# Weight conversion in a fused attention, DFT and MLP kernel: the sign as a byte written by ScalarE, the exponent change in ScalarE's scale

## The chip, the cores and the metric

The kernel runs on one core of one Trainium2 chip. The metric is the device time of one execution in microseconds (us); lower is better. The engines that the text speaks of are PE (TensorE: matmuls, with PEld for the loading of its stationary operand), DVE (VectorE), ACT (ScalarE), POOL (GpSimd) and SP (SyncE, which issues the DMAs).

## The reference

Four batches of causal attention with 12 heads give `x`. The real part of a two-dimensional DFT of `x` is added to it, each row is normalised, and an MLP with 768 inputs and 3072 hidden units follows, with a residual.

```
attn_out = softmax(mask(q @ k.T / 8)) @ v            # 4 x 12 heads, 448 x 64
x   = attn_out as [4, 448, 768]
u   = x + real(fft(fft(x, axis=1), axis=2))
un  = (u - mean(u)) / sqrt(var(u) + 1e-6)
out = u + relu(un @ w_ch1) @ w_ch2   # w_ch1 [768, 3072], w_ch2 [3072, 768]
```

The two weight arrays reach the kernel as 64-bit floats, and it makes 32-bit floats of them itself.

## The kernel before, in words

**Stages.** From 0 to about 240 us PE works through 24 pairs of heads, and in between through the DFT, the normalisation and the transposes of the batches that are ready. From about 240 us it works through the MLP: two groups of 896 tokens, each with 12 chunks of 256 hidden units. For a chunk the first product (`f1`, matmuls of 448 columns, written `h`) is followed by the second (`f2`, matmuls of 384 columns, written `o`), and the plan weaves `f2` of a chunk with `f1` of the next. Each matmul is done three times, with operands that are split into a high and a low part. In the first group a plain chunk has 72 matmuls in `f1`, a chunk from number 5 on, counted from 0, has 63 (a recursion with seven products, `fast`), and each has 84 in `f2`. After six matmuls of `f2` DVE adds the PSUM tile into an accumulator in SBUF (L1168); there are 14 such adds for a chunk of the first group, called a **round** here.

**The weights.** The first group converts them, in 48 pieces of 128 x 768 numbers, two of `w_ch1` and two of `w_ch2` for a chunk. A piece arrives by DMA as pairs of 32-bit words, tile `w`: `w[:, :, 0]` the low word and `w[:, :, 1]` the high word of each 64-bit float. Five operations in `weights()` make 32-bit floats of it: ACT writes the magnitude of the high word, read as a 32-bit float, to `w32` (L742), and ACT replaces the low word by its top three bits, from its top byte (L746). DVE joins those bits and the sign bit in the high word (L752), caps the magnitude and changes its exponent (L758), and shifts it by three and joins the rest (L762). The result stays in `w32`. From it come high and low parts: for `w_ch2` by ACT (L775, tile `w2h`) and POOL (L779); for `w_ch1` by `split` and `combine` (`w1` and `ws` tiles, L811 and L824 on DVE or POOL, casts at L335 on ACT). The second group loads what the first has stored.

**What sets the order.** A planner (`Plan.order`) takes a list of units, each with an engine or a choice of engines, a cost and a priority, and writes out a fixed order for every engine before anything runs; engines then go through their lists in order and wait on semaphores. Units with two engines named, such as L811, L824, L905, L930 and L1108 (DVE or POOL), go where the planner thinks that they end first. A cost or a dependency that is changed anywhere can therefore move instructions everywhere behind it. PSUM tiles come from eight banks; the `c` copies (L335, ACT or DVE) take an `h` product out of its bank, and the product that follows into that bank waits for them.

Of the kernel before, what the change touches and what calls it, by code (L numbers as in the profile page):

```python
# [9 lines left out]
F32 = mybir.dt.float32  # L10
F32R = mybir.dt.float32r
BF16 = mybir.dt.bfloat16
U32 = mybir.dt.uint32
U8 = mybir.dt.uint8
ACTF = mybir.ActivationFunctionType
ALU = mybir.AluOpType
AX = mybir.AxisListType.X
# [2 lines left out]
B, H, S, D = 4, 12, 448, 64  # L20
# [28 lines left out]
SLOW, BIAS = 1.5, dict(S=-300, V=-100, G=-500)  # L49
BIG = float(2 ** 30)  # L50
W_SCALE = 2.0 ** -112
W_HIGH = float(np.uint32((1151 << 20) - 1).view(np.float32))
ORDER = (
    [2 * j for j in range(R)]
    + [2 * j + 1 for j in range(R)]
# [20 lines left out]
class Plan:  # L76
# [11 lines left out]
    def add(self, eng, cost, prio, fn, rd=(), wr=(), phase=None):  # L88

        n = len(self.units)  # L90
        deps = sorted({w for r in rd for w in self.writers[r]})
        for x in wr:
            self.writers.setdefault(x, []).append(n)
        for x in set(z[:2] for z in (*rd, *wr)):
            self.uses.setdefault(x, []).append(n)
        many = isinstance(eng, tuple)
        self.units.append(dict(
            n=n, engs=dict(zip(eng, cost)) if many else {eng: cost}, many=many, prio=prio, fn=fn, deps=deps, phase=phase,
            new=sorted({z[:2] for z in wr if z[0] in self.bufs}, key=str)))
# [165 lines left out]
def tile_kernel(ctx, tc, qk, vv, w1, w2, cc, cd, cs, out):  # L265
    nc = tc.nc if tc else None
    T = {}
# [42 lines left out]
    add = plan.add  # L310
# [7 lines left out]
    def dve(n, rate=0.96):  # L318
        return 69 + n / rate
# [4 lines left out]
    def acts(n):  # L324
        return 94 + n * 0.833
# [62 lines left out]
    def attend(i):  # L388
# [50 lines left out]
        for k, rows in enumerate(rows_):  # L439
# [23 lines left out]
            for y, r in enumerate(rows):  # L463
                for h, ps in enumerate(banks):
# [7 lines left out]
                    def f(ps=ps, c0=at[r], n=n, rr=rr):  # L472
                        nc.scalar.activation(  # L473
                            out=T[pb][:, PO[rr]:PO[rr] + n], in_=T[ps][:, c0:c0 + n], func=ACTF.Exp, scale=-1.0,
                            bias=T[mn][:, rr:rr + 1], accum_out=T[sm][:, rr:rr + 1])
# [247 lines left out]
    def weights(j, nm, half, p0):  # L723
        g, c = items[j]
        id_ = (j, half)
        if twice(j):
            if half and not (nm == "1" and kept(j)):
                w = ("w", (nm, j))

                def f():  # L730
                    nc.sync.dma_start(out=wide(w), in_=dr["wf"][int(nm) - 1, c])
                add("D", dma(786432), p0 - 3000, f, rd=[("wf", nm, c)], wr=[w], phase="W")
            return
        w, w32, wh, wl = ("w", (nm, j, half)), ("w32", (nm, j, half)), ("w2h", id_), ("w2l", id_)

        def f():
            src = (w1 if nm == "1" else w2)[2 * c + half]
            nc.sync.dma_start(out=T[w], in_=src.bitcast(U32).rearrange("p (a b) -> p a b", b=2))
        add("D", dma(786432), p0 - 3000, f, rd=[("go", W_FROM)] if j == 0 else [], wr=[w], phase="W")

        def f():
            nc.scalar.activation(out=T[w32].bitcast(F32), in_=T[w][:, :, 1].bitcast(F32), func=ACTF.Abs)  # L742
        add("S", acts(768) + 71, p0, f, rd=[w], wr=[(*w32, 0)], phase="W")

        def f():
            nc.scalar.activation(  # L746
                out=T[w][:, :, 0], in_=T[w].bitcast(U8)[:, :, 3], func=ACTF.Copy, scale=1 / 32, bias=-31 / 64)
        add("S", acts(768) + 75, p0 + 1, f, rd=[w], wr=[(*w, 1)], phase="W")

        def f():  # L750
            x = T[w][:, :, 1]
            nc.vector.scalar_tensor_tensor(  # L752
                out=x, in0=x, scalar=0x80000000, in1=T[w][:, :, 0], op0=ALU.bitwise_and, op1=ALU.bitwise_or)
        add("V", dve(768) + 4, p0 + 2, f, rd=[(*w, 1), (*w32, 0)], wr=[(*w, 2)], phase="W")

        def f():
            x = T[w32].bitcast(F32)
            nc.vector.tensor_scalar(out=x, in0=x, scalar1=W_HIGH, scalar2=W_SCALE, op0=ALU.min, op1=ALU.mult)  # L758
        add("V", dve(768, 1.92) + 4, p0 + 2, f, rd=[(*w32, 0)], wr=[(*w32, 1)], phase="W")

        def f():
            nc.vector.scalar_tensor_tensor(  # L762
                out=T[w32], in0=T[w32], scalar=3, in1=T[w][:, :, 1], op0=ALU.logical_shift_left, op1=ALU.bitwise_or)
        add("V", dve(768) + 4, p0 + 4, f, rd=[(*w32, 1), (*w, 2)], wr=[(*w32, 4)], phase="W")

        if not (nm == "1" and kept(j)):
            def f():
                nc.sync.dma_start(out=dr["wf"][int(nm) - 1, c, :, half], in_=T[w32].bitcast(F32))
            add("D", dma(393216), p0 + 5, f, rd=[(*w32, 4)], wr=[("wf", nm, c)], phase="W")

        if nm == "2":
            wide_lo = (*w32, 4)

            def f():
                nc.scalar.copy(out=T[wh], in_=T[w32].bitcast(F32))  # L775
            add("S", acts(768), p0 + 5, f, rd=[wide_lo], wr=[wh], phase="L")

            def f():
                nc.gpsimd.tensor_tensor(out=T[wl], in0=T[w32].bitcast(F32), in1=T[wh], op=ALU.subtract)  # L779
            add("G", gps(768), p0 + 6, f, rd=[wide_lo, wh], wr=[wl], phase="L")  # L780
# [613 lines left out]
```

## Time and profile before

| | before |
|---|---|
| median of 3 runs | 944.24 us (944.07 to 949.7) |
| span of the profiled execution | 942.7 us |
| PE busy | 903.4 us (96%) |
| DVE busy | 796.9 us (85%) |
| POOL busy | 627.6 us (67%) |
| ACT busy | 545.3 us (58%) |
| HBM traffic | 178 GB/s over the span |

The profiled execution's span runs from its first to its last instruction and lies 1.5 us under the median of the runs; no other time is given for that execution. A busy share says nothing of which engine is late at a given moment: that is read by stage, from windows, waits and the chain of work that ended last.

### The profile page before, as it was taken

To read this page: it belongs to the slowest core of one execution; us is meant where nothing else is said; L and a number is where in the kernel's file an instruction comes from. 1 tells how busy PE (TensorE), PEld (TensorE's weight loads), DVE (VectorE), ACT (ScalarE), POOL (GpSimd) and SP (SyncE) were. 2 spreads that over 40 slices of the span, in tenths; PEclk is the share of its full clock that TensorE was granted. 3 is DMA by queue.
4 is the path that set the end of the run, shared out by engine and by line. 5 is a ranking of instruction groups with operands and counts; after the bars stand their busy time and mean duration, and the time that the engine had idled before them with its cause. 6 is when DMAs were issued, how large, how long until landed. Compare 5 with 4: busy or idle time off the path is not lost.

```text
span 942.7 us, 16159 instructions
## 1 busy us (share of the span) xinstructions
PE 903.4 (96%) x5636; PEld 805.8 (85%) x5636; DVE 796.9 (85%) x1330; ACT 545.3 (58%) x1300; POOL 627.6 (67%) x648
## 2 busy tenths in 40 slices
PE   7999999999799999999999988999999999999998
PEld 4667668777688999988989887998999999999998
DVE  6889999898897887999998999997788676666668
ACT  6999798988644444545454456645454453444442
POOL 4798698884642222443543337799999898887886
PEclk9999999999899999999999999999999999999999
DMA  7624624615569556758777668665123444444403
GB/s 274 220 88 170 183 77 138 164 45 180 149 210 345 171 208 224 245 196 292 277 275 256 214 217 295 210 217 174 48 68 118 129 139 136 141 145 136 149 1 117
DMA packets 67537, 165.84 MB, mean 176 GB/s; under 512 B 18976, under 2 KB 31904, under 8 KB 67360
## 3 DMA queue, kind: packets, MB, share of 16 engines
q1 hardware_dynamic: 67456, 164.82, 52.8%
q8 instruction: 44, 0.72, 0.3%
q14 instruction: 37, 0.30, 0.1%
HBM read 112.89 MB, written 54.74 MB: 178 GB/s over the span
## 4 chain that ended last, share of the span: by engine, by line
PE 60%; DVE 21%; POOL 6%; issue 6%; ACT 6%; DMA 1%; SPq 0%; POOLq 0%; DVEq 0%; ACTq 0%
PE h L978 22%; PE o L1180 16%; PE o L1219 8%; PE x L531 4%; PE pt L505 3%; PE sc L457 3%; DVE acc L1168 3%; DVE w L762 3%; DVE w L752 2%; ACT p L473 2%; DVE w L811 1%; DVE w L758 1%; DVE mn L469 1%; DVE ws L824 1%; DVE hl L1015 1%
## 5 line engine op out<-in xcount | busy, mean ns | idle before, releaser
L1168 DVE TENSOR_TENSOR acc<-o,acc 128x384 f32<-128x384 f32 x444 | 236.8, 552 | 79.9 <-PE o L1180 56.3
L1219 PE MATMUL o<-w2l,hh 128*128 128x384 f32 x336 | 113.6, 338 | 1.4 <-POOL w2l L779 1.3
L1219 PE MATMUL o<-w2h,hh 128*128 128x384 f32 x336 | 113.3, 337 | 1.6 <-DVE acc L1168 1.6
L1219 PE MATMUL o<-w2h,hl 128*128 128x384 f32 x336 | 113.1, 337 | 0.0
L779 POOL TENSOR_TENSOR w2l<-w,w2h 128x768 fp32r<-128x768 f32 x24 | 49.7, 2071 | 78.6 <-ACT w2h L775 71.6
L494 POOL TENSOR_TENSOR p<-p,ri 128x128 f32<-128x128 f32 (+3 forms) x113 | 79.1, 729 | 22.0 <-DVE ri L485 18.1
L811 POOL TENSOR_TENSOR w<-w,w 128x384 fp32r<-128x384 f32 x33 | 39.7, 1203 | 60.1 <-ACT w L335 59.1
L978 PE MATMUL h<-u11h,w 128*128 128x448 f32 x174 | 64.8, 380 | 3.4 <-ACT u11h L335 3.0
L1219 PEld LDWEIGHTS o<-w2l,hh 128*128 128x128 f32 x336 | 63.1, 188 | 4.4 <-POOL w2l L779 2.6
L1219 PEld LDWEIGHTS o<-w2h,hh 128*128 128x128 f32 x336 | 63.2, 188 | 4.2 <-DVE acc L1168 2.3
L978 PE MATMUL h<-u22h,w 128*128 128x448 f32 x174 | 63.2, 371 | 3.2 <-DVE c L1051 3.2
L1180 PE MATMUL o<-w2h,hh 128*128 128x384 f32 x288 | 65.1, 339 | 0.3 <-DVE acc L1168 0.3
L978 PE MATMUL h<-u12h,w 128*128 128x448 f32 x174 | 64.1, 370 | 0.0
L1219 PEld LDWEIGHTS o<-w2h,hl 128*128 128x128 f32 x336 | 63.2, 188 | 0.0
L978 PE MATMUL h<-u21h,w 128*128 128x448 f32 x174 | 63.0, 367 | 0.0
L1180 PE MATMUL o<-w2l,hl 128*128 128x384 f32 x288 | 62.4, 338 | 0.4 <-DVE acc L1168 0.4
L505 PE MATMUL pt<-cst,p 128*128 128x128 f32 (+1 forms) x384 | 56.9, 281 | 2.6 <-ACT p L492 1.9
L505 PEld LDWEIGHTS pt<-cst,p 128*128 128x128 f32 (+1 forms) x384 | 41.4, 139 | 16.8 <-issue 5.7
L335 ACT COPY c<-h 128x448 f32<-128x448 f32 x57 | 30.1, 529 | 44.1 <-PE h L978 40.2
L867 POOL TENSOR_TENSOR w2h<-w,w2h 128x384 fp32r<-128x384 f32 x43 | 45.8, 1065 | 14.6 <-ACT w2h L335 14.6
L473 ACT ACTIVATE p<-sc,mn 128x448 f32<-128x448 f32 (+3 forms) x96 | 50.4, 525 | 7.6 <-DVE mn L469 6.7
L1180 PEld LDWEIGHTS o<-w2h,hh 128*128 128x128 f32 x288 | 52.1, 188 | 2.6 <-DVE acc L1168 0.6
(212 smaller groups left out, 2999.7 us busy)
## 6 DMA issues: line engine op xcount, KB each, us to landing
w<-in_w_dram SPq DMA_DIRECT2D x48, 768.0 KB, 4.9
wp<-w SPq DMA_DIRECT2D x49, 384.0 KB, 3.5
w<-wp SPq DMA_DIRECT2D x49, 384.0 KB, 3.1
wf<-w SPq DMA_DIRECT2D x34, 384.0 KB, 2.9
w<-wf SPq DMA_DIRECT2D x17, 768.0 KB, 4.3
raw<-in_qk_dram SPq DMA_DIRECT2D x23, 480.0 KB, 3.8
us<-und SPq DMA_DIRECT2D x45, 224.0 KB, 4.2
v<-in_vv_dram SPq DMA_DIRECT2D x24, 256.0 KB, 2.9
```

What stands on the lines that cost most here:

```text
L335: nc.scalar.copy(out=out, in_=in_)
L473: nc.scalar.activation(out=T[pb][:, PO[rr]:PO[rr] + n], in_=T[ps][:, c0:c0 + n], func=ACTF.Exp, scale=-1.0, bias=T[mn][:, rr:rr + 1], accu ...
L494: nc.gpsimd.tensor_tensor(out=x, in0=x, in1=z.to_broadcast([128, KE[r]]), op=ALU.mult)
L505: nc.tensor.transpose(T[ps][0:m, 128 * k:128 * k + 128], T[pb][:, PO[r] + 128 * c:PO[r] + 128 * c + m], T["cst", 0][:, 0:128])
L531: nc.tensor.matmul(out=T[xps][64 * h:64 * h + 64, q0:q0 + w], lhsT=T[v][0:kk, c, h * D:(h + 1) * D], rhs=T[src][0:kk, s0 + h * sd:s0 + h * ...
L779: nc.gpsimd.tensor_tensor(out=T[wl], in0=T[w32].bitcast(F32), in1=T[wh], op=ALU.subtract)
L811: (nc.gpsimd if eng == "G" else nc.vector).tensor_tensor(out=T[z][:, 1], in0=src(), in1=T[z][:, 0], op=ALU.subtract)
L867: (nc.gpsimd if eng == "G" else nc.vector).tensor_tensor(out=T[z][:, 384:768], in0=src(), in1=T[z][:, 0:384], op=ALU.subtract)
L978: nc.tensor.matmul(out=T[ps][:, 0:S], lhsT=a[:, t], rhs=x[:, t], start=start and k == 0, stop=stop and k == 8, skip_group_check=True)
L1168: nc.vector.tensor_tensor(out=x, in0=T[ps][:, 0:384], in1=x, op=ALU.add)
L1180: nc.tensor.matmul(out=T[ps][:, 0:384], lhsT=hpart(j, h, a)[:, k * 128:k * 128 + 128], rhs=T[z][:, 384 * b:384 * b + 384], start=start and ...
L1219: nc.tensor.matmul(out=T[ps][:, 0:384], lhsT=T[a][:, m, k * 128:(k + 1) * 128], rhs=w[:, sl], start=(m == 0 and z == 0), stop=(m == 1 and ...
```

## The change

The operation at L752 on DVE goes. In its place ACT gets a third operation for each piece: it multiplies the high word, read as a 32-bit float, by 2^-20 where positive and by 2^80 where negative, and writes the result as a signed byte. A positive number rounds to 0 and a negative one saturates at the byte with only its top bit set. That byte goes into the top byte of the low word, which then holds sign and low bits together. The first ACT operation takes the exponent factor as its scale, DVE's cap loses the multiplication, and DVE's last operation joins from `w[:, :, 0]`. The ScalarE function `Prelu`, which was not in the kernel before, does the new operation.

```diff
+I8 = mybir.dt.int8
 W_SCALE = 2.0 ** -112
-W_HIGH = float(np.uint32((1151 << 20) - 1).view(np.float32))
+W_TOP = float(np.uint32((1151 << 20) - 1).view(np.float32)) * W_SCALE
+SIGN_SCALE, SIGN_ALPHA = 2.0 ** -20, 2.0 ** 100
...
-            nc.scalar.activation(out=T[w32].bitcast(F32), in_=T[w][:, :, 1].bitcast(F32), func=ACTF.Abs)
+            nc.scalar.activation(out=T[w32].bitcast(F32), in_=T[w][:, :, 1].bitcast(F32), func=ACTF.Abs, scale=W_SCALE)
         add("S", acts(768) + 71, p0, f, rd=[w], wr=[(*w32, 0)], phase="W")
...
         def f():
-            x = T[w][:, :, 1]
+            nc.scalar.activation(
+                out=T[w].bitcast(I8)[:, :, 3], in_=T[w][:, :, 1].bitcast(F32), func=ACTF.Prelu, scale=SIGN_SCALE, alpha=SIGN_ALPHA)
+        add("S", acts(768) + 75, p0 + 1, f, rd=[w, (*w, 1)], wr=[(*w, 2)], phase="W")
+
+        def f():
+            x = T[w32].bitcast(F32)
+            nc.vector.tensor_scalar(out=x, in0=x, scalar1=W_TOP, scalar2=None, op0=ALU.min)
+        add("V", dve(768, 1.92) + 4, p0 + 2, f, rd=[(*w32, 0)], wr=[(*w32, 1)], phase="W")
+
+        def f():
             nc.vector.scalar_tensor_tensor(
-                out=x, in0=x, scalar=0x80000000, in1=T[w][:, :, 0], op0=ALU.bitwise_and, op1=ALU.bitwise_or)
-        add("V", dve(768) + 4, p0 + 2, f, rd=[(*w, 1), (*w32, 0)], wr=[(*w, 2)], phase="W")
-
-        def f():
-            x = T[w32].bitcast(F32)
-            nc.vector.tensor_scalar(out=x, in0=x, scalar1=W_HIGH, scalar2=W_SCALE, op0=ALU.min, op1=ALU.mult)
-        add("V", dve(768, 1.92) + 4, p0 + 2, f, rd=[(*w32, 0)], wr=[(*w32, 1)], phase="W")
-
-        def f():
-            nc.vector.scalar_tensor_tensor(
-                out=T[w32], in0=T[w32], scalar=3, in1=T[w][:, :, 1], op0=ALU.logical_shift_left, op1=ALU.bitwise_or)
+                out=T[w32], in0=T[w32], scalar=3, in1=T[w][:, :, 0], op0=ALU.logical_shift_left, op1=ALU.bitwise_or)
         add("V", dve(768) + 4, p0 + 4, f, rd=[(*w32, 1), (*w, 2)], wr=[(*w32, 4)], phase="W")
```

Above L742 the changed kernel's lines stand two lower, from L763 on one lower: L744 is the magnitude, L748 the low bits, L753 the new operation, L759 the cap and L763 the join.

The planner writes a new order. Here are DVE's rows of the order before where the 33rd and 34th piece, of `w_ch2`, are converted (at 485 to 494 us in the trace); a name behind `<-` is what is read, and numbers tell tiles of one name apart (`acc` rows are the adds, `c` rows sums of `h` products, `hl` a low part).

```order
L752 SCALAR_TENSOR_TENSOR w<-w 128x768
L758 TENSOR_SCALAR w_6388<-w_6388 128x768
L1051 TENSOR_TENSOR c<-h,c 128x448
L762 SCALAR_TENSOR_TENSOR w_6388<-w_6388,w 128x768
L758 TENSOR_SCALAR w_6415<-w_6415 128x768
L1168 TENSOR_TENSOR acc_4502<-o_6351,acc_4502 128x384
L752 SCALAR_TENSOR_TENSOR w<-w 128x768
L1015 SCALAR_TENSOR_TENSOR hl<-c,hh 128x448
L762 SCALAR_TENSOR_TENSOR w_6415<-w_6415,w 128x768
```

The same two pieces on DVE in the changed kernel.

```order
L759 TENSOR_SCALAR w_6365<-w_6365 128x768
L812 TENSOR_TENSOR w_6374<-ws,w_6374 128x384
L763 SCALAR_TENSOR_TENSOR w_6365<-w_6365,w 128x768
L1169 TENSOR_TENSOR acc_4507<-o_6335,acc_4507 128x384
L1052 TENSOR_TENSOR c<-h,c 128x448
L1169 TENSOR_TENSOR acc_4509<-o_6358,acc_4509 128x384
L1169 TENSOR_TENSOR acc_4509<-o_6384,acc_4509 128x384
L1169 TENSOR_TENSOR acc_4511<-o_6403,acc_4511 128x384
L759 TENSOR_SCALAR w_6414<-w_6414 128x768
L1169 TENSOR_TENSOR acc_4511<-o_6426,acc_4511 128x384
L763 SCALAR_TENSOR_TENSOR w_6414<-w_6414,w 128x768
```

Both pieces have two operations in place of three there, and the second one now stands behind four adds more. ACT's rows of the order before at the same place:

```order
L742 ACTIVATE w_6388<-w 128x768
L742 ACTIVATE w_6415<-w 128x768
L746 ACTIVATE w<-w 128x768
L775 CAST w2h<-w_6388 128x768
L1009 ACTIVATE hh<-c 128x448
L335 COPY c<-h 128x448 x2
L775 CAST w2h<-w_6415 128x768
```

ACT at the same place in the changed kernel.

```order
L744 ACTIVATE w_6365<-w 128x768
L337 CAST w_6374<-ws 128x384
L776 CAST w2h<-w_6365 128x768
L744 ACTIVATE w_6414<-w 128x768
L748 ACTIVATE w<-w 128x768
L337 COPY c<-h 128x448
L753 ACTIVATE w<-w 128x768
L1010 ACTIVATE hh<-c 128x448
L776 CAST w2h<-w_6414 128x768
L337 COPY c<-h 128x448
```

The new operation of the second piece (L753) stands between the first `c` copy and the cast of that piece, and the second `c` copy stands behind both.

## Rows read from the trace of the kernel before

**Rows 1.** By stretch: length; PE, PEld, DVE, ACT, POOL busy (count); PEclk; DMA share, GB/s.

```profile
88.00:240.00 152.00, 146.45 (x1345) 111.15 (x1341) 136.79 (x275) 133.60 (x403) 116.06 (x154) 1.00 0.46 135
240.00:300.00 60.00, 52.89 (x307) 48.73 (x308) 54.60 (x78) 30.80 (x57) 31.35 (x29) 0.94 0.71 227
300.00:395.00 95.00, 95.00 (x507) 90.81 (x506) 78.14 (x122) 46.13 (x69) 26.18 (x18) 1.00 0.62 212
395.00:640.00 245.00, 229.91 (x1207) 215.59 (x1206) 231.90 (x327) 125.56 (x218) 128.66 (x94) 1.00 0.72 249
640.00:760.00 120.00, 118.95 (x617) 112.01 (x618) 96.05 (x156) 60.40 (x139) 113.50 (x112) 0.99 0.31 102
```

**Rows 2.** Who waited for whom, PE, 395 to 640 us: total, times, longest.

```profile
PE h L978 <- ACT c L335: 9.3, 7, 2.8
PE h L978 <- DVE c L1051: 3.2, 3, 1.7
```

**Rows 3.** The chain of work that ended last, 484 to 494 us: start, length, what.

```profile
485.12 0.91 ACT w L742
...
487.11 0.87 DVE w L752
487.97 0.47 DVE w L758
...
488.90 0.96 DVE w L762
...
489.88 0.83 ACT w2h L775
...
491.19 0.43 ACT c L335
...
491.66 2.08 PE h L978 x9
```

**Rows 4.** The same chain, PE at its full pace.

```profile
336.00 3.71 PE h L978 x18
339.71 2.08 PE o L1219 x12
```

**Rows 5.** The same stretch: matmuls of L978, of L1219, then DVE's L752.

```profile
395.00:640.00 245.00, 119.04 (x514) 94.55 (x514) 1.00 0.72 249
...
395.00:640.00 245.00, 132.32 (x693) 122.06 (x692) 1.00 0.72 249
...
395.00:640.00 245.00, 28.84 (x26) 1.00 0.72 249
```

**Rows 6.** DVE's groups of instructions, 300 to 640 us: busy, mean ns, idle before.

```profile
L1168 DVE TENSOR_TENSOR acc<-o,acc 128x384 f32<-128x384 f32 x166 | 86.9, 548 | 17.3 <-PE o L1219 16.9
L762 DVE SCALAR_TENSOR_TENSOR w<-w,w 128x768 uint32<-128x768 uint32 x41 | 45.4, 1108 | 0.1
L752 DVE SCALAR_TENSOR_TENSOR w<-w 128x768 uint32<-128x768 uint32 x40 | 43.2, 1081 | 1.2 <-ACT w L742 0.9 <-ACT w L746 0.2
L758 DVE TENSOR_SCALAR w<-w 128x768 f32<-128x768 f32 x40 | 27.1, 679 | 0.6 <-ACT w L742 0.6
L1015 DVE SCALAR_TENSOR_TENSOR hl<-c,hh 128x448 fp32r<-128x448 f32 x21 | 19.3, 918 | 2.4 <-ACT hh L1009 2.3
L811 DVE TENSOR_TENSOR w<-ws,w 128x384 fp32r<-128x384 f32 x23 | 18.3, 827 | 0.9 <-ACT w L335 0.9
```

**Rows 7.** ACT's groups of instructions, whole span: its two operations on a piece.

```profile
L746 ACT ACTIVATE w<-w 128x768 uint32<-128x768 uint8 x48 | 43.8, 913 | 12.9 <-DMA w<-in_w_dram 10.4 <-DVE t2l L905 2.5
L742 ACT ACTIVATE w<-w 128x768 f32<-128x768 f32 x48 | 43.6, 909 | 8.8 <-DMA w<-in_w_dram 3.1 <-POOL ws L824 3.0 <-DVE ws L824 1.8
```

**Rows 8.** Who waited for whom, ACT, 395 to 640 us.

```profile
ACT w2h L775 <- DVE w L762: 19.7, 11, 2.7
ACT w L335 <- DVE w L762: 10.8, 4, 3.7
```

**Rows 9.** One instruction line, L762: durations min/median/max, first and last start.

```profile
L762 DVE SCALAR_TENSOR_TENSOR w<-w,w x48: 941/949/2586, 137.7 to 612.2; 128x768 uint32<-128x768 uint32 x48
```

## The prediction

> **What bounds the kernel now.** I read the busy time by stretch first [rows 1]. From 300 to 395 us PE has no idle time, with DVE at 78.1 of 95 us. From 395 to 640 us PE idles 245 - 229.9 = 15.1 us while DVE is busy 231.9 of 245 us (95%), ACT 125.6 (51%) and POOL 128.7 (53%). From 640 us on no piece is converted (the last starts at 612.2 us [rows 9]), PE idles 1.0 us in 120 and POOL is the full engine (113.5 of 120). So if the change can give time, it is between 395 and 640 us, and to a small part before 300.
>
> PE's busy time hides part of a loss, since the ends of its matmuls are modelled; so I count matmuls. At full pace 18 matmuls of f1 take 3.71 us and 12 of f2 take 2.08 us [rows 4], 0.206 and 0.1733 us each. From 395 to 640 us there are 514 and 693 [rows 5]: 105.9 + 120.1 = 226 us. PE loses 245 - 226 = 19 us there. That is the most that this stretch can give.
>
> The waits of PE there name ACT's `c` copies, 9.3 us in 7 waits, and DVE's sums, 3.2 us [rows 2]. ACT itself is not full; the chain shows why it is late [rows 3]: magnitude on ACT (0.91 us), then L752, L758 and L762 on DVE, then ACT's cast of the result, then the `c` copy behind that cast, then PE. ACT goes through its list in order, and with its casts it waits 19.7 + 10.8 = 30.5 us for L762 [rows 8]. DVE is the late engine, and through ACT's queue it holds up PE.
>
> **What the change removes.** 48 times L752, and 38 of them in DVE's rounds 2 to 12, counted from the first add (a round is 14 adds). I compare the rounds before and after by the order: how often each line stands in a round, times its mean from DVE's groups between 300 and 640 us, of which the heaviest are shown [rows 6]. What PE needs for a round is 72 x 0.206 + 84 x 0.1733 = 29.4 us in a plain chunk and 63 x 0.206 + 14.6 = 27.5 us in a fast one. As an example, the worst round before holds 14 adds (7.7 us), six whole conversions (6 x (1.081 + 0.679 + 1.108) = 17.2), and five `hl`, three `c` sums and five operations on weight halves (10.1): 35.0 us, 7.5 more than PE needs. In the changed order that round has three caps and three joins (5.4 us), and is 24.6 us.
>
> Rounds 2 to 12 before, in us: 26.0, 30.3, 32.8, 29.7 (plain), 30.5, 33.3, 24.0, 35.0, 29.9, 28.3, 26.2 (fast). Sum 326; what stands over PE's need, round by round, is 0 + 1.0 + 3.4 + 0.4 + 3.0 + 5.8 + 0 + 7.5 + 2.4 + 0.8 + 0 = 24.3 us. After: 25.3, 24.6, 29.2, 27.0, 27.2, 27.1, 27.2, 24.6, 30.3, 30.5, 25.1. Sum 298; over PE's need 2.8 + 3.0 = 5.8 us.
>
> So 38 x 1.081 = 41.1 us leave DVE, and the planner gives 13 us back: four more of L811, six of L905, two of L1015, fewer of L930 and so on, some of it taken over from POOL, some from other rounds. The overhang falls by 24.3 - 5.8 = 18.5 us. The trace shows 19 us of loss for 24.3 of overhang, 0.78 of it, since queues and free banks carry PE over a short lateness; 0.78 x 18.5 = 14.5 us. DVE still has 298 of the 310 us that PE needs, so single waits will stay, and I take **-13 us**, with 0 and -19 as ends.
>
> **What it adds.** ACT gets 48 operations. The trace has no byte as output. The nearest rows are the two operations on the same piece, 909 ns with words on both sides and 913 ns reading bytes eight bytes apart [rows 7]; the first has the same input, the second the same stride at byte width. I take 0.91 us: 44 us in all. The lower end is ACT's cast of a whole piece, 0.83 us [rows 3]; the upper end, for a byte that costs a second pass over the word, is twice 0.91. In the stretch 26 pieces [rows 5] would add 23.7 us to ACT's 125.6: 149 of some 232 us, 64%. Hidden by ACT's idle time, so **0** on the path, as long as ACT's waits for DVE shrink too; the 30.5 us that it waits for L762 are more than what is added. If that cover is gone, the `c` copies pay (first rival). The operation stands between low bits and join, so the join has one operation of ACT more and one of DVE less ahead of it; DVE waited for ACT's two operations only 1.2 us at L752 and 0.6 us at L758 from 300 to 640 us [rows 6]. Scale and a cap without its multiplication take no more instructions: 0. No DMA is added or moved past another on purpose; the weight tile `w` is still freed by the join, and comes free no later.
>
> [...]
>
> **Elsewhere.** Before 300 us eight pieces are converted, and the planner orders attention and DFT anew from there on. PE idles 5.6 us from 88 to 240 us and 7.1 us from 240 to 300 us, where the granted clock is 0.94 as a mean [rows 1]. New order can win or lose some of these: I take 0, from -4 to +4. From 640 us on the second group starts with POOL full: I take -1 for a smoother start, from -3 to +2.
>
> **Sum.** -13 + 0 - 1 = -14 us; 942.7 - 14 = 928.7 us of span, and with the 1.5 us between span and median 930.2 us.
>
> **The rivals.**
>
> *The `c` copies wait for ACT instead (no change).* PE's largest wait is for these copies [rows 2], and each may now find a 0.91 us operation ahead of it on ACT: in the order after, one stands between the two copies at the place shown. Seven fast chunks have three such copies each, 21 in all; with half an operation, 0.45 us, for each, 9.5 us of the 13 come back: 944.2 - 4.5 = 940. For it: the name in the waits. Against it: ACT is idle half the time, and it was late because of DVE.
>
> *The join waits for the byte (slower).* If the byte output takes twice as long, or ACT comes to it late, DVE stands in L763 with adds queued behind it, and PE lacks banks. DVE gains 28 us in 38 pieces, so a wait of 28 / 38 = 0.74 us for each join undoes the gain, and from there on it is slower. At 1.3 us for each join DVE needs 298 + 49 = 347 us against 326 before: 0.78 x 21 = +16, so 960. Against it: the two neighbours cost the same whatever their input's width.
>
> *All of the loss goes (much faster).* L762 takes 949 ns as a median, 1108 ns as a mean and up to 2586 ns [rows 6, 9]: DVE's operations stretch where POOL works beside them. With a two-input operation less for each piece both engines stretch less, and the 5.8 us of overhang vanish as well. Then -19 in the stretch, -4 before 300 us and -2 behind it: 919. [...]
>
> *The function costs table loads.* [...] The order of the changed kernel has a single table load on ACT, as before, so I give this nothing.
>
> **How the numbers follow.** Forecast, 924 to 936: 0.53. Much faster, below 924: 0.15. No change, 936 to 953: 0.24. Slower, above 953: 0.08. A measurement of this kernel tells about 1% (9.4 us) from no change, so faster means below 934.8: 0.15 and nine tenths of the forecast, 0.48, are 0.63; same 0.29; slower 0.08. The range leaves out the slower case and the ends of the first and second: 919 to 943.
>
> **What would show it.** In the profile after: DVE's busy time from 395 us to the last conversion falls by some 20 us or more and its share of the stretch stays below 95%; PE idles less than 6 us there; ACT's new group has 48 instructions near 0.91 us; ACT's wait for the join falls well below 30 us; PE's wait for `c` copies is below 4 us. Wrong if the byte takes over 1.3 us, if DVE waits for ACT at the join or the cap for over 10 us in all, if the waits for `c` copies stay at 9 us, or if the order anew costs more than 5 us before 300 us.

## The result and the profile after

The changed kernel takes 956.12 us (median of 4 runs, 953.41 to 960.36) against 944.79 us of the kernel before in the same comparison; the ratio is 1.0109 with a 95% interval of 1.0072 to 1.0146. The forecast was 930.2 us: the sign was wrong. The profiled execution has a span of 958.6 us. It is the slowest of the four, so its rows differ from those of the kernel before by 15.9 us, where the medians differ by 11.3.

By stretch, the same columns as [rows 1] (length; PE, PEld, DVE, ACT, POOL busy with counts; granted clock; DMA share, GB/s), changed kernel:

```profile
88.00:240.00 152.00, 148.51 (x1328) 112.94 (x1328) 137.34 (x283) 136.74 (x398) 111.29 (x148) 0.98 0.41 126
240.00:300.00 60.00, 51.37 (x313) 45.20 (x313) 48.32 (x77) 38.10 (x64) 29.89 (x32) 0.91 0.66 201
300.00:395.00 95.00, 92.96 (x481) 88.64 (x482) 67.82 (x103) 69.93 (x81) 24.46 (x16) 0.96 0.64 223
395.00:640.00 245.00, 229.23 (x1180) 215.21 (x1179) 205.98 (x302) 167.38 (x233) 102.34 (x75) 0.97 0.68 237
640.00:760.00 120.00, 118.44 (x619) 110.82 (x618) 98.74 (x156) 59.15 (x136) 115.72 (x116) 1.00 0.35 124
```

DVE is relieved as forecast: 206.0 us of the stretch from 395 to 640 us in place of 231.9. But PE does 1180 matmuls there and not 1207. ACT went from 125.6 to 167.4 us, 42 us more, where the forecast had 24. The granted clock is below that of [rows 1] in each of the first four stretches. Over the whole span its mean is 0.980, before 0.995: 958.6 x 0.020 - 942.7 x 0.005 = 14 us of full speed, an estimate from above, since PE idles in part of that time. PE's idle time is hardly longer than before over the whole span (958.6 - 918.5 = 40.1 us, before 942.7 - 903.4 = 39.3). So in this execution most of the loss stands in PE's busy time, and the low clock makes a good part of it. The clock is no measure of the loss in general: e4, below, has a mean clock of 0.987 and a span of 942.5 us, as short as before, and e19 has 0.984 and idles 962.1 - 909.8 = 52.3 us.

A part of the 15.9 us does not come from the change. PE's first 300 matmuls, kernel before and changed kernel:

```profile
0.00:42.00 42.00, 36.41 (x300) 23.21 (x300) 30.10 (x73) 31.77 (x105) 24.32 (x37) 1.00 0.79 271
0.00:45.80 45.80, 42.44 (x300) 27.06 (x300) 31.02 (x73) 32.01 (x105) 23.26 (x37) 1.00 0.70 247
```

The changed kernel is 3.8 us late at that point, and its first piece is converted at 91.8 us only (88.0 before). Executions of one order differ by as much: e4, with the changed kernel's order, has its first 300 in 42.2 us, and e3, with the order before, in 44.2.

The groups of instructions of the conversion, whole span, changed kernel (those of the kernel before are in [rows 6, 7]):

```profile
L753 ACT ACTIVATE w<-w 128x768 int8<-128x768 f32 x48 | 94.0, 1958 | 0.8
L763 DVE SCALAR_TENSOR_TENSOR w<-w,w 128x768 uint32<-128x768 uint32 x48 | 49.8, 1037 | 23.3 <-ACT w L753 23.1
L748 ACT ACTIVATE w<-w 128x768 uint32<-128x768 uint8 x48 | 43.6, 909 | 3.6 <-DMA w<-in_w_dram 3.5
L744 ACT ACTIVATE w<-w 128x768 f32<-128x768 f32 x48 | 43.5, 908 | 8.3 <-DVE acc L1169 4.5 <-POOL w2l L780 2.2 <-DVE ws L825 0.9
```

The byte takes 1.958 us, more than twice its two neighbours on the same piece. DVE waits 23.1 us for it at the join. Who waited for whom, PE from 395 to 640 us (total, times, longest), beside [rows 2]:

```profile
PE h L979 <- ACT c L337: 12.0, 7, 4.4
PE o L1220 <- POOL w2l L780: 2.3, 2, 1.3
```

ACT's waits for the join in the same stretch, beside [rows 8]:

```profile
ACT w2h L776 <- DVE w L763: 9.7, 11, 1.7
ACT w L337 <- DVE w L763: 8.0, 4, 4.5
```

So ACT no longer waits as long for DVE (17.7 us where it was 30.5), DVE's own late sums are gone from PE's waits, and yet the `c` copies are later: 12.0 us, before 9.3. The longest of these waits shows why. ACT in order of time (start, length, what, idle time before):

```profile
566.16 1.92 ACT L753 ACTIVATE w<-w 128x768 int8<-128x768 f32 x1
567.83 0.62 ACT L337 COPY c<-h 128x448 f32<-128x448 f32 x1
```

PE at the same place:

```profile
568.50 0.74 PE L979 MATMUL h<-t3h,w 128*128 128x448 f32 x1 [4.39 <-ACT c L337]
...
572.85 0.74 PE L979 MATMUL h<-t4h,w 128*128 128x448 f32 x1 [0.62 <-ACT c L337]
...
576.22 0.52 PE L1220 MATMUL o<-w2h,hh 128*128 128x384 f32 x1
...
578.24 0.34 PE L1220 MATMUL o<-w2h,hh 128*128 128x384 f32 x1
```

And the windows around it, with the columns of the first table:

```profile
568.00:578.00 10.00, 8.88 (x26) 7.73 (x27) 2.76 (x4) 4.01 (x7) 1.96 (x2) 0.54 0.51 181
578.10:588.30 10.20, 10.20 (x57) 9.90 (x56) 7.00 (x13) 7.07 (x8) 1.02 (x1) 1.00 0.34 117
```

The copy that PE needs stands right behind a byte operation on ACT. PE idles for 4.39 us; in that idle time, at 567 us, its granted clock falls from 1.00 to 0.50, and it stays there until 577 us (0.54 on the mean of the first window, 1.00 in the second, and `o` matmuls of 0.52 us that take 0.34 behind it): 26 matmuls in 10 us where the next 10.2 us hold 57. PE counts as busy for 8.88 of those 10 us. This wait of 4.4 us is paid twice, once as idle time and once as slow matmuls. The byte is not the whole of that wait: two magnitudes, the low bits and a cast stand ahead of it on ACT from 562.64 us on. The same matmul in e4, which has the same order and a word of 0.91 us in place of the byte:

```profile
553.12 0.48 PE L979 MATMUL h<-t3h,w 128*128 128x448 f32 x1 [2.81 <-ACT c L337]
```

### The profile page after: what moved, and what is told of

Read it like the earlier page. It is cut to its first block, busy times and chain, and to the rows that moved or that the text cites. A ratio compares the mean times of both kernels' runs of the same rounds, so it can differ in the third digit from the quotient of the medians.

```text
span 958.6 us, 16135 instructions
## 1 busy us (share of the span) xinstructions
PE 918.5 (96%) x5636; PEld 817.0 (85%) x5636; DVE 764.2 (80%) x1306; ACT 624.8 (65%) x1333; POOL 605.4 (63%) x639
## 5 line engine op out<-in xcount | busy, mean ns | idle before, releaser
L780 POOL TENSOR_TENSOR w2l<-w,w2h 128x768 fp32r<-128x768 f32 x24 | 46.7, 1950 | 92.4 <-ACT w2h L776 84.7
L496 POOL TENSOR_TENSOR p<-p,ri 128x128 f32<-128x128 f32 (+3 forms) x114 | 76.8, 704 | 34.7 <-DVE ri L487 30.2
L753 ACT ACTIVATE w<-w 128x768 int8<-128x768 f32 x48 | 94.0, 1958 | 0.8
L763 DVE SCALAR_TENSOR_TENSOR w<-w,w 128x768 uint32<-128x768 uint32 x48 | 49.8, 1037 | 23.3 <-ACT w L753 23.1
L1220 PEld LDWEIGHTS o<-w2h,hh 128*128 128x128 f32 x336 | 64.6, 192 | 3.9 <-ACT w2h L776 1.7
L868 POOL TENSOR_TENSOR w2h<-w,w2h 128x384 fp32r<-128x384 f32 x45 | 48.6, 1080 | 15.1 <-ACT w2h L337 15.1
L812 POOL TENSOR_TENSOR w<-w,w 128x384 fp32r<-128x384 f32 x24 | 30.4, 1268 | 42.7 <-ACT w L337 33.4
```

The lines of the kernel that those rows point to most:

```text
L496: nc.gpsimd.tensor_tensor(out=x, in0=x, in1=z.to_broadcast([128, KE[r]]), op=ALU.mult)
L753: nc.scalar.activation(out=T[w].bitcast(I8)[:, :, 3], in_=T[w][:, :, 1].bitcast(F32), func=ACTF.Prelu, scale=SIGN_SCALE, alpha=SIGN_ALPHA)
L763: nc.vector.scalar_tensor_tensor(out=T[w32], in0=T[w32], scalar=3, in1=T[w][:, :, 0], op0=ALU.logical_shift_left, op1=ALU.bitwise_or)
L812: (nc.gpsimd if eng == "G" else nc.vector).tensor_tensor(out=T[z][:, 1], in0=src(), in1=T[z][:, 0], op=ALU.subtract)
L868: (nc.gpsimd if eng == "G" else nc.vector).tensor_tensor(out=T[z][:, 384:768], in0=src(), in1=T[z][:, 0:384], op=ALU.subtract)
L1220: nc.tensor.matmul(out=T[ps][:, 0:384], lhsT=T[a][:, m, k * 128:(k + 1) * 128], rhs=w[:, sl], start=(m == 0 and z == 0), stop=(m == 1 and ...
```

## Experiments

Four questions: what the byte costs and why; what it costs on the path; what VectorE's relief is worth; and what the new order is worth by itself. For the last two it matters that the planner writes the engines' lists from its own costs. Kernels of which only an operand differs keep the order of every engine, row by row, and are compared without that question; others get an order of their own, in which some units with a choice of two engines also go to the other one.

**e1_forms: what makes the operation long.** The changed kernel, the third operation in four forms for 12 pieces each.

```diff
+            if nm == "1" and half == 0:    # Prelu -> byte 3
+            elif nm == "1":                # Copy  -> byte 3
+            elif half == 0:                # Prelu -> word 0 (uint32)
+            else:                          # Prelu -> upper half word (int16)
```

> The changed kernel in its own order, with the third ScalarE operation in four forms, 12 pieces each: Prelu to a byte as it is; Copy to a byte (sign lost); Prelu to the whole 32-bit word (low bits lost); Prelu to the upper 16-bit half of the word. Theory A, the byte (an output narrower than a word) is what doubles the time: the byte forms at 1.96 us, the word at 0.91, the half word at one or the other. Theory B, the function doubles it (Prelu, with its two slopes, goes over the data at half the pace): all three Prelu forms at 1.96 us, Copy to a byte at 0.91.

Groups of instructions on ACT, whole span:

```profile
L761 ACT ACTIVATE w<-w 128x768 int16<-128x768 f32 x12 | 23.5, 1960 | 0.2
L755 ACT ACTIVATE w<-w 128x768 int8<-128x768 f32 x12 | 23.5, 1956 | 0.2
L757 ACT ACTIVATE w<-w 128x768 int8<-128x768 f32 x12 | 23.4, 1950 | 0.2
L759 ACT ACTIVATE w<-w 128x768 uint32<-128x768 f32 x12 | 11.0, 916 | 0.2
```

Not the function: a copy to a byte takes 1.950 us, `Prelu` 1.956. Not the conversion to an integer either: a whole word takes 0.916 us. What the three long forms have in common is that only part of a word is written; the half word takes 1.960 us, as long as the byte.

**e5_forms2: is it part of a word as such, or the gap?** Four other forms: 768 bytes side by side, 768 half words side by side, one byte in each of 768 words side by side (every four bytes), and a byte read and written every eight bytes. The excerpt is shortened: `flat(w)` stands for the tile's words as one row.

```diff
+  out=flat(w).bitcast(I8)[:, 0:768]              # side by side
+  out=flat(w).bitcast(I16)[:, 0:768]             # side by side
+  out=flat(w)[:, 0:768] as bytes, every 4th      # pitch 4
+  out=T[w].bitcast(U8)[:, :, 3], in_=...[:, :, 7]  # pitch 8, byte in, byte out
```

> The changed kernel in its own order, the third ScalarE operation in four forms with junk as output, 12 pieces each: Prelu to 768 bytes that lie side by side; Prelu to 768 half words that lie side by side; Prelu to one byte of each of 768 words side by side; Copy of a byte to a byte, both eight bytes apart. Theory of the part of a word (an element that fills a word only in part and has no neighbour in the same write costs a second pass): side by side 0.91 us, a byte in each word 1.96 us, byte to byte 1.96 us. Rival, the width of the output type costs as such: all four at 1.96 us.

```profile
L762 ACT ACTIVATE w<-w 128x768 uint8<-128x768 uint8 x12 | 23.5, 1962 | 0.2
L759 ACT ACTIVATE w<-w 128x768 int8<-128x768 f32 x12 | 13.1, 1092 | 0.2
L755 ACT ACTIVATE w<-w 128x768 int8<-128x768 f32 x12 | 10.8, 902 | 0.2
L757 ACT ACTIVATE w<-w 128x768 int16<-128x768 f32 x12 | 10.8, 900 | 0.2
```

Part words side by side take 0.90 us, about as long as the whole ones of e1 (0.916), and part words eight bytes apart 1.96 us. At a pitch of four bytes it is 1.09 us, where I had expected the long time. So the long time came with a part word and a gap together: 1.96 us at a pitch of eight bytes, 1.09 at four. What makes it long, no run shows.

**e2_true_cost: does the plan fail because it has the wrong price?** The planner's cost of the third operation is raised to what the trace shows.

```diff
-        add("S", acts(768) + 75, p0 + 1, f, rd=[w, (*w, 1)], wr=[(*w, 2)], phase="W")
+        add("S", acts(768) + 1125, p0 + 1, f, rd=[w, (*w, 1)], wr=[(*w, 2)], phase="W")
```

> The changed kernel, but the planner is told 1.86 us for the third ScalarE operation in place of 0.81. If most of the loss comes from an order that was planned for a shorter operation (theory of the plan), DVE's waits for it at the join fall from 23 us to under 6 us and the time to 944 to 949 us. If ScalarE simply has no room for 48 times 1.96 us in front of the copies that PE waits for (theory of the queue), the waits change place and the time stays at 953 to 960 us.

955.32 us, ratio 1.0098 (1.0068 to 1.0128). DVE's waits from 300 to 640 us:

```profile
DVE w L763 <- ACT w L753: 6.8, 10, 1.6
```

The wait at the join falls from 23.1 to 6.8 us, and the time stays where it was; PE's wait for `c` copies, 11.3 us from 300 to 645 us, stays as well. A plan with the right price does not give the time back here. Its order is another one, so what the wait at the join costs by itself is not shown.

**e3_scale_only: the part that should cost nothing.** The kernel before, with the exponent moved into ACT's scale and a cap without multiplication.

```diff
-  ... func=ACTF.Abs)
+  ... func=ACTF.Abs, scale=W_SCALE)
-  ... scalar1=W_HIGH, scalar2=W_SCALE, op0=ALU.min, op1=ALU.mult)
+  ... scalar1=W_TOP, scalar2=None, op0=ALU.min)
```

> One part alone: the kernel before with the exponent factor in the first ScalarE operation's scale and a cap without its multiplication on VectorE; the sign stays where it was, and the order is the same as before, row by row. By all theories no change: both operations keep 0.91 and 0.55 us as a median, 943 to 947 us.

944.25 us, ratio 0.9988 (0.9968 to 1.0008): nothing, as forecast. The order is that of the kernel before.

**e4_word: the changed kernel with the operation at the price I forecast.** Order and waits of the changed kernel; the third operation writes a whole word.

```diff
-  out=T[w].bitcast(I8)[:, :, 3], in_=..., func=ACTF.Prelu, ...
+  out=T[w].bitcast(mybir.dt.int32)[:, :, 0], in_=..., func=ACTF.Prelu, ...
```

> The changed kernel in its own order, word for word, but the third ScalarE operation writes the whole low word as a 32-bit integer (0 or the sign bit alone) in place of one byte of it; the three low bits are lost, so the weights are cut to 21 bits. The operation then takes what the forecast priced, 0.91 us. Theory of the size (only this term was wrong): 924 to 936 us, with DVE's waits at the join under 6 us and the granted clock back above 0.99. Rival, the new order itself costs: 942 us or more, with the stalls before 300 us still there.

944.11 us, ratio 0.9993 (0.9977 to 1.0009): the theory of the size missed, and its rival, that the new order itself costs, has the time right. Window, and PE's waits from 300 to 645 us:

```profile
395.00:640.00 245.00, 235.99 (x1229) 221.89 (x1228) 217.19 (x315) 145.04 (x243) 115.05 (x86) 0.99 0.72 249
```

```profile
PE h L979 <- ACT c L337: 8.4, 8, 2.8
```

Against the changed kernel in the same order this is 12.0 us less: the byte's price. But even at 0.91 us the forecast gain is not there. PE does 22 matmuls more than before in the stretch (1229, 1207), some 4 us of work, and the `c` copies are waited for nearly as long as before.

**e7_no_low: no added work on ACT.** As e4, and the low bits' operation is left out, so that ACT has two operations for each piece as before and DVE its whole relief; the order is new.

```diff
-                out=T[w][:, :, 0], in_=T[w].bitcast(U8)[:, :, 3], func=ACTF.Copy, scale=1 / 32, bias=-31 / 64)
-        add("S", acts(768) + 75, p0 + 1, f, rd=[w], wr=[(*w, 1)], phase="W")
```

> The word form of the third ScalarE operation, and the second one (the three low bits) left out: weights cut to 21 bits, ScalarE with two operations for a piece as in the kernel before, VectorE with two in place of three, order planned anew. If VectorE's relief is what pays and ScalarE's third operation costs little (theory of the size), about as fast as with three word operations, 922 to 934 us. If ScalarE's queue counts at 0.91 us already, over 5 us faster than that kernel.

940.11 us, ratio 0.9932 (0.9908 to 0.9956): under e4 by 4.0 us in the medians and 5.8 in the ratios, so slower than the first theory had and at the edge of the second (over 5 us). How much of it the new order makes is open.

**e8_both: the added work without the relief.** The kernel before with the byte operation added, and L752 kept.

```diff
+        add("S", ..., f, rd=[w, (*w, 1)], wr=[(*w, 6)], phase="W")   # Prelu -> byte
-        add("V", dve(768) + 4, p0 + 2, f, rd=[(*w, 1), (*w32, 0)], ...
+        add("V", dve(768) + 4, p0 + 2, f, rd=[(*w, 1), (*w, 6), (*w32, 0)], ...
```

> The kernel before with the third ScalarE operation added and nothing taken from VectorE (the sign is written twice, the result is the same): the price of the 1.96 us operation without the relief. If the relief is worth the 14 us of the forecast, this is slower than the changed kernel by about as much, 966 to 975 us. If the relief is worth nothing, 953 to 960 us.

987.53 us, ratio 1.0441 (1.0415 to 1.0467), slower than I expected. With both engines loaded, taking L752 away (that is, going on to the changed kernel, in another order) is worth 31 us, more than any two orders of one form differ below (20 us). That speaks for a real relief of DVE. It does not give its size: the edit also makes L752 wait for the byte, 10.3 us in 14 waits from 300 to 640 us, a wait that the kernel before does not have.

**Where in the span.** I counted the matmuls of f1 and f2 in order of time and read when a given one starts. The 200th starts at 304.0 us before, at 308.6 in e4 and at 314.6 in the changed kernel; the 1900th follows the 700th after 245.6, 240.0 and 250.5 us. So the changed kernel loses 10.6 us before 315 us, 3.8 of them at the start, and 4.9 behind; e4 wins its loss back later. Counted from PE's 300th matmul (42.0, 42.2 and 45.8 us) the 200th of f1 and f2 is 4.4 us late in e4 and 6.8 in the changed kernel. The next three kernels split the pieces by that: the first eight, which are converted before 300 us, and the 40 others.

```diff
+        first = (nm == "1" and j <= 2) or (nm == "2" and j == 0)
+        if first:
...
+        else:
...
```

Under `first` e9 and e10 have the operations of the kernel before and e11 the byte; under `else` e9 has the word, e10 the byte and e11 the operations of the kernel before. All three lists are new; e9 and e10 have the same one.

> The first eight pieces, which are converted before 300 us, in the form of the kernel before (with the sign's operation on VectorE); the other 40 as in e4, with a whole word in place of the byte (the low three bits of the weights are left out there). Theory A, the early loss comes from the third ScalarE operation on the first eight pieces: e4 lost 4.6 us before 305 us and won 5.6 between 400 and 645 us; without the loss 938 to 941 us. Theory B, any new order of the start costs it, whichever operations the first pieces have: the start stays 4 to 5 us late, 943 to 946 us. In the trace: start of the 200th matmul of f1 and f2 at 304 us (A) or near 308.6 (B).

> The first eight pieces in the form of the kernel before, the other 40 with the byte as in the changed kernel; nothing is left out. Theory A: the 8 to 10 us that the changed kernel loses before 315 us vanish, its loss behind that stays: 946 to 949 us. Theory B: as slow as the changed kernel, 953 to 958 us. Start of the 200th matmul at 304 to 306 us (A) or 312 to 315 us (B).

> The counterpart: the first eight pieces with the byte, the other 40 in the form of the kernel before; nothing is left out. Theory A: only the early loss, 8 to 10 us: 951 to 955 us. Theory B, the loss comes with the later pieces: 943 to 947 us.

e9_late_word takes 934.72 us, ratio 0.9877 (0.9846 to 0.9908); e10_late_byte 948.7, ratio 1.0032 (1.0005 to 1.0059); e11_early_byte 952.73, ratio 1.0067 (1.0041 to 1.0092). The 200th matmul starts at 305.6, 306.4 and 313.4 us. That is what theory A said of all three, and e9 was faster still; as each has a new order, it is shown for these orders alone. e9's windows and its wait for `c` copies from 300 to 645 us:

```profile
240.00:300.00 60.00, 52.20 (x311) 47.48 (x310) 52.74 (x77) 33.57 (x64) 32.95 (x30) 0.94 0.72 228
...
395.00:640.00 245.00, 239.62 (x1270) 227.58 (x1270) 215.34 (x317) 152.33 (x258) 124.90 (x96) 1.00 0.73 256
```

```profile
PE h L1008 <- ACT c L338: 4.2, 6, 1.2
```

Window of e10, which has e9's order and the byte (its profiled execution, 945.19 us, is the fastest of its ten):

```profile
395.00:640.00 245.00, 231.85 (x1220) 218.80 (x1219) 208.76 (x307) 172.14 (x249) 116.26 (x89) 0.99 0.72 249
```

e9 is the picture that I had forecast: 1270 matmuls in the stretch, PE idle 5.4 us, `c` waits near 4 us, a gain of 1.2%. In the same order the byte takes 50 of the 63 matmuls away again.

**e12_pitch4: a form with nothing left out that avoids the gap.** For the 40 later pieces the low bits go to 768 words side by side, and the sign's byte into every fourth byte. Not in the excerpt: the first operation keeps the sign (`Copy` in place of `Abs`), the sign is read from its result, the low bits wait for it, since they overwrite high words, and the cap waits for the sign.

```diff
-  out=T[w][:, :, 0], in_=T[w].bitcast(U8)[:, :, 3], func=ACTF.Copy, ...
+  out=low(w), in_=T[w].bitcast(U8)[:, :, 3], func=ACTF.Copy, ...
-  out=T[w].bitcast(I8)[:, :, 3], in_=T[w][:, :, 1].bitcast(F32), func=ACTF.Prelu, ...
+  out=low(w) as bytes, every 4th, in_=T[w32].bitcast(F32), func=ACTF.Prelu, ...
-  ... scalar1=W_TOP, scalar2=None, op0=ALU.min)
+  ... scalar1=W_TOP, scalar2=-W_TOP, op0=ALU.min, op1=ALU.max)
```

> The first eight pieces as before; for the other 40 a form with nothing left out that avoids bytes eight apart: the first ScalarE operation keeps the sign, the low bits are written as 768 words side by side, the sign's byte is read from the scaled words and written every four bytes (1.09 us in e5 in place of 1.95), the cap bounds on both sides, the join is the same. ScalarE carries some 0.18 us per piece more than in e9 and 0.86 us less than in e10. By the line between e9 (934.7) and e10 (948.7): 936 to 940 us, faster than both kernels. If what counts in e10 is not the byte's time but that the cap and the join wait for one ScalarE operation more, the cap's new wait for the sign makes it as slow as e10 or slower: 947 us or more. The operation itself: 1.05 to 1.15 us; if the input's stride counted in e5, another value.

952.29 us, ratio 1.0061 (1.0044 to 1.0078): the 936 to 940 us missed, and the time is that of the other case, 947 us or more. The operation is as short as hoped, and the cap now waits for it (16.1 us), as the groups show; whether that wait or the new order costs the time, this run does not tell:

```profile
L785 ACT ACTIVATE w<-w 128x768 int8<-128x768 f32 x40 | 43.1, 1077 | 0.7
...
L791 DVE TENSOR_SCALAR w<-w 128x768 f32<-128x768 f32 x40 | 26.0, 651 | 17.3 <-ACT w L785 16.1 <-issue 1.0
```

**e13_cap_waits: is that wait the cause?** e9, where the planner is told that the cap needs the third operation.

```diff
-            add("V", dve(768, 1.92) + 4, p0 + 2, f, rd=[(*w32, 0)], wr=[(*w32, 1)], phase="W")
+            add("V", dve(768, 1.92) + 4, p0 + 2, f, rd=[(*w32, 0), (*w, 2)], wr=[(*w32, 1)], phase="W")
```

> e9 with one thing more: the cap also waits for the third ScalarE operation (a whole word, 0.91 us; the low three bits of the later 40 pieces are left out, as in e9). If e12 was slow since its cap waits for the third operation, this one loses as well, with ScalarE's work unchanged: 942 us or more, and VectorE waits at the cap for over 8 us. If the wait at the cap costs little, it stays within 2 us of e9, 933 to 937 us, and e12 was slow for its 1.08 us operation.

955.12 us, ratio 1.0092 (1.0062 to 1.0122): slow as in the first case, but not for the reason that I gave. The edit changes the plan alone; the waits on the chip follow the data, and the cap waits on nothing but the first operation (L773), 4.2 us in all:

```profile
DVE w L788 <- ACT w L773: 4.2, 6, 1.4
```

The same work with the same needs, written in another order (and with a few units on another engine), takes 20 us more than e9. That made the order itself the question, for every comparison above in which it differs.

**e14 to e19: the order alone.** Three forms of the conversion, each in two further orders: the planner's cost of the cap is 1 ns less, or the planner believes that the cap waits for the low bits. Neither changes an operand or a wait on data. A few units with a choice go to another engine (DVE has 1306 instructions in e4, 1299 in e16 and 1294 in e17), so what is drawn again is order and engine.

```diff
-        add("V", dve(768, 1.92) + 4, p0 + 2, f, rd=[(*w32, 0)], ...
+        add("V", dve(768, 1.92) + 3, p0 + 2, f, rd=[(*w32, 0)], ...            # 1 ns
+        add("V", dve(768, 1.92) + 4, p0 + 2, f, rd=[(*w32, 0), (*w, 1)], ...   # believed wait
```

> The kernel before, with one number of the planner's changed: the cap's cost is 1 ns less. Every instruction, operand and wait on data is the same, only the written order of the engines' lists is drawn anew (651 of PE's rows stand elsewhere). Theory O, an order drawn anew is worth up to 10 us by itself, and the order before is a lucky one: 947 to 958 us. Theory W, the order follows the work and a small shift is worth little: 942 to 946 us.

> The kernel before, where the planner believes that the cap waits for the low bits too; on the chip the same instructions with the same waits on data, in another order. Theory O: 947 to 960 us, and 3 us or more from the one with 1 ns. Theory W: 942 to 946 us.

> e4 (all 48 pieces with the whole word, 0.91 us; the low three bits of the weights are left out) with the cap's cost in the plan 1 ns less. Theory O: anywhere from 930 to 955 us, over 3 us from e4's 944.1. Theory W: 942 to 946 us.

> e4 (low three bits left out), where the planner believes that the cap waits for the low bits too. Theory O: anywhere from 930 to 955 us; with e4 and the run before it the mean lies some 10 us under the mean of the kernel before in its three orders, which would be the relief of VectorE without the draw. Theory W: 942 to 946 us.

> The changed kernel in the order of e16 (cap's cost in the plan 1 ns less): against e16 only the third operation's output differs, a byte for a word; nothing is left out. If the byte's price is a term of its own, 12 to 14 us as in the two pairs before: 960 to 964 us. If it is what a given order makes of it, anything from 949 to 975 us.

> The changed kernel in the order of e17 (the planner believes that the cap waits for the low bits): byte's price as a term of its own 961 to 965 us. The mean of the changed kernel over its three orders is then near 959, against 952.5 of the kernel before over its three: slower by some 7 us without the luck of the order; if VectorE's relief were nothing it would be 12 or more.

| ratio to the kernel before (95% interval), median us | form before | third operation a word | a byte |
|---|---|---|---|
| plan as it is | 1, by definition | e4: 0.9993 (0.9977 to 1.0009), 944.1 | changed kernel: 1.0109 (1.0072 to 1.0146), 956.1 |
| cap 1 ns less | e14: 1.0076 (1.0053 to 1.0098), 953.8 | e16: 1.0033 (1.0010 to 1.0056), 949.0 | e18: 1.0130 (1.0055 to 1.0206), 961.3 |
| believed wait | e15: 1.0134 (1.0107 to 1.0161), 959.2 | e17: 1.0058 (1.0031 to 1.0085), 949.9 | e19: 1.0129 (1.0060 to 1.0198), 963.7 |
| mean | 1.0070 | 1.0028 | 1.0123 |

Word and byte of a row have one order; the form before has another in each row. Medians of different runs compare less well than ratios, as each ratio has the kernel before measured beside it: 944.8 to 946.4 us beside these kernels, 948.7 beside e18 and e19. Theory O holds: the kernel before loses 7 to 13 us by being written in another order, and its own is the best of its three. The 10 us that e17 expected between the means of word and form before came out as 0.42%, 4 us.

The byte's price against the word is 12.0, 12.3 and 13.8 us by the medians, and 14.0 in e9 and e10; by the ratios it is 11.0, 9.2, 6.7 and 14.6 us (1.16, 0.97, 0.71 and 1.55%). The first and the last are clear of their intervals; those of e16 and e18 touch, and those of e17 and e19 overlap. The traces say the same in all four: from the 700th to the 1900th matmul of f1 and f2 the byte takes 10.5, 6.2, 7.0 and 9.6 us more than the word. So it is a term of its own, and its size depends on the order. Some 7 us of e19's profiled loss against e17 lie behind its 1900th matmul, where no piece is converted any more.

## Why the prediction was wrong

**The byte was mis-sized.** "I take 0.91 us" went by two neighbours, one with the same input and one that reads bytes eight apart [rows 7]. Neither writes part of a word. It measured 1.958 us, just over the upper end that the text gave, twice 0.91 for "a second pass over the word", so the end was right and the choice wrong. The step that mattered is the one behind it, "Hidden by ACT's idle time, so **0** on the path": ACT is busy for 167 of 245 us, 68%, and still the byte costs 12 us against a word in an unchanged order (7 to 15 us in the four orders tried). ACT goes through its list in order, so its idle time hides the operation only where that time lies. Here the operation stands ahead of `c` copies, which PE waits for (12.0 us, 8.4 with the word).

**The relief was over-sized.** The term of -13 us took DVE's overhang as the whole cause of PE's loss, late `c` copies included, and the third operation as free. In e4, at the price that was forecast, PE still waits 8.4 us for these copies, before 9.3. From the 700th to the 1900th matmul the word took 240.0, 240.0 and 242.7 us in its three orders, against 245.6 of the kernel before (246.4 and 254.6 in its other two): 3 to 6 us against the run that the forecast started from, 8 us between the means. Only e7 and e9 reach 232.3, the 13.3 us of the forecast: once without the added work on ACT, and once in one order with it. The sum of rounds thus gave what a good order can get. The planner's next list does not get it as a rule.

**"Elsewhere" was outside its bounds.** I took 0, from -4 to +4, before 300 us. The 200th matmul starts 4.6 us late with the word and 10.6 with the byte, 4.4 and 6.8 when counted from PE's 300th. Counted so, it is 1.3 us early to 0.4 late with the first eight pieces in the form of before, in four kernels of three orders (e9, e10, e12, e13), 3.7 to 9.7 us late with the word on them in three, and 5.1 to 10.7 with the byte in four (e11 too). The form before itself is 7.4 us late in e14 and 2.9 early in e15, so one order in three loses it without the change; that ACT's added work makes the loss more likely is what the runs show, no more.

**What I had not put in the sum.** The text compared the two orders round by round, and gave no price to drawing an order anew. The order before is a good one: its other two cost 0.76 and 1.34%. By the means of the table the +1.09% are made of +0.70 (the good order is given up), -0.42 (the word in place of L752), +0.95 (the byte in place of the word) and -0.14 (the changed kernel's order is better than its form's mean). The third comes from equal orders and has one sign in all of them. The first two are means of three draws that scatter by 0.7% and 0.3%; the sign of the second is not settled.

**The rivals.** The first, that `c` copies wait for ACT, named the right place and priced it at half an operation of 0.91 us; at the byte's length PE waits 12.0, 11.4 and 14.6 us for them (changed kernel, e18, e19) and 8.4, 8.9 and 10.2 with the word. The longest in the changed kernel (4.39 us) comes with the low clock shown above; not each does: behind a wait of 2.78 us in the kernel before, at 585.8 us, the granted clock stays at 1.00, and so it does in the changed kernel behind one of 2.44 us, at 602.6 us. The second, that the join waits, came near in time (960, at 1.3 us for each join). The wait is there, 23.1 us in 22 of 48 joins, but e2 cut it to 6.8 us without a gain, in an order of its own. In e9 and e10 both waits rise together with the byte, so how the 14 us divide between the join and the `c` copies stays open. The third, that all of the loss goes, came out nowhere: e9, the fastest, takes 934.7 us and not 919, and why its order is that good stays open. What it started from, that DVE's operations stretch where POOL works beside them, is in the trace of the kernel before: the ten of the 48 L762 that take 1.30 to 2.59 us each run beside a POOL instruction, and of the other 38, at 0.94 to 0.96 us, only four do; that POOL is the cause, no run shows. The mean over the span did fall, from 1128 ns (L762) to 1037 (L763). Table loads stayed at nothing: the traces of both kernels and of e1 hold one ACT_TABLE_LOAD each (1.28 us).

Of the signs of being wrong that the text named, three came true: the byte over 1.3 us, DVE's wait over 10 us, and `c` waits not below 9 us. The fourth, over 5 us lost before 300 us, is not clear: at 297 us f1 and f2 are 5.3 us late, 3.8 of it from the start, and another 5 us are lost between 297 and 307 us.

No kernel with nothing left out beat the kernel before. e9, with the low three bits of 40 pieces left out, is 1.2% faster; a form that writes sign and low bits at that price was not found.

## What to carry to other kernels

Price a new operation by a row with the same output (width and pitch), not only the same input (here 0.912 us for a word and 1.958 for a byte, from one input); if there is none, the far end belongs into the range with real weight. An engine that goes through its list in order covers added work only where its idle time lies (ACT was busy 68% of the stretch here, and the byte still cost 12 us), so look at what stands right behind the added instruction and who waits for that. And where a planner writes the order from costs, measure how far the time moves when only the order is drawn again, before a change of about 1% is believed or blamed: here it moved by 0.8 and 1.3% in the form before for a nanosecond in one cost or a dependency that isn't there (0.4 and 0.65% with the word, 0.2% with the byte), and by 2% between e9 and e13.

## What the runs showed of the hardware

An ACT operation on 128 x 768 elements that wrote a byte or a half word every eight bytes took 1.95 to 1.96 us (e1 and e5; the byte with `Prelu` and `Copy`, from 32-bit floats and from bytes; the half word with `Prelu` alone). A byte at a pitch of four bytes took 1.08 to 1.09 us (e12, e5), a byte or a half word side by side 0.90 (e5), and a whole word every eight bytes 0.91 to 0.92 (e4, e1).

PE's lost time stood in its busy time as well: in the changed kernel the granted clock was 0.50 from the wait of 4.39 us that ends at 568.5 us until 577 us, and 1.00 from 578.1 to 588.3 us. In its profiled execution the changed kernel has the same 5636 matmuls and about the same idle time as the kernel before, and 15.1 us more of busy time.

The start of an execution varied without a change of order: PE's first 300 matmuls take 42.0 and 44.2 us in two kernels of one order (before, e3), and 42.2 and 45.8 in two of another (e4, changed kernel).
